# An attention block beside a feed-forward block on one core: truer delays and two new rules in the program that orders the instructions

## The chip, the cores and the metric

The kernel runs on one core of a Trainium2 chip. The metric is device time in microseconds (us). Times are medians of several runs; a run is called fast or slow by its time and by the granted clock of TensorE (the share of its full clock that it was given), which each run records. Ratios are computed as the mean time of one kernel's fast runs over that of the other kernel's fast runs of the same rounds, so they are not quite the ratio of the medians quoted here.

## The reference, cut to what matters

```python
xn = layernorm(x)                              # x: 2048 x 640
q  = xn @ wq   (32 heads of 20)                # one key and one value head for all 32
s  = q k^T * 20**-0.5;  p = softmax(s)         # 32 x 2048 x 2048 scores
A  = (p v) @ wo
B  = relu(xn @ w1 + b1)**2 @ w2 + b2           # F = 1536
out = x + A + B
```

The 134 million exponentials of the softmax are the large item. Most are done by ScalarE; a part is done by VectorE and GpSimd with a bit trick, to relieve ScalarE.

## The kernel before

The order of the instructions is not written by hand. When the kernel is built, a program places every operation on its engine with an assumed duration and assumed delays, always choosing what can start next, and writes the resulting fixed order with semaphores. So wrong figures in this *order model* cannot make a wrong result; they make a poor order. The model is only the ordering program's belief; every time in this text is from the chip.

These terms are used below:

- A **step** is one exponential: ScalarE reads 128x1024 scores from two banks of PSUM, the memory that TensorE writes its products into (`ps` in the trace lines). Its **score pair** (`QK`) is the two TensorE products that filled them. There are two pairs of banks, so pair j must wait until exponential j-2 has been read out, and exponential j must wait for pair j.
- A **set** is a key tile that VectorE handles instead of ScalarE, with 4 score products (`DQK`). Such a product is meant to **ride** directly behind a score pair, because both use a 20-row strip of the array (`20*128` in the trace lines); what changing to other work costs is measured below.
- **Column groups** are all other TensorE work (PV products, which multiply the probabilities by the values; projections; feed-forward): groups of four 32-column products side by side. A **zero-fill** is a group that adds zeros; it is meant to keep the array active (e9 below measures what two such groups were worth at one place).
- A **block** is four heads for 512 queries (32 blocks). Its PV products add up in one bank. When a block ends, this bank is closed until VectorE has transposed it (0.71 us a transpose, from the page).

The parts that the change and the argument touch:

```python
class Op:
    ...
    def ready(self):                          # when the order model believes it can start
        t = 0.0
        for d in self.deps:
            ...
            t = max(t, d.fin + (self.lat1 if self.lat1 is not None and d.eng == "PE" else d.lat))
        return t                              # d.lat: 0.2 from TensorE, 2.2 from a DMA, else 0.06
...
    def make_act(st_):                        # the exponential of a step
        ...
        return Op(f"ACT{st_['j']}", "ACT", 0.064 + 0.4267 * n, [...], deps)
...
    def make_dqk(heads):                      # heads: row groups that the pair just placed occupies
        ...
        h = ([h for h in s["left"] if h not in heads] or s["left"])[0]
        ...
        return Op(f"DQK{d}", "PE", 0.02 if heads else 0.215, [...], ..., mode="R"), s, h, bank
...
    while True:                               # place the next operation
        ...
        for u in active.values():             # "misc units": projections, feed-forward, in chunks
            ...
            consider("PE", 2, o, ("misc", u))
        ...
        if pick[2].eng == "PE":
            ...
            while pick[0] > free["PE"] + 0.1 + (...) and act_ops and pe_use(min(pick[0], free["PE"] + 1.0)) < 1.0:
                ...                           # place a zero-fill, if a bank is open for it
```

Note `0.02 if heads else 0.215`: the model counts a riding product as nearly free, also where `h` is a row group that the pair occupies, that is, where no other head of the set was left. I call that a **colliding rider**. A rider placed after other work, not directly behind its pair, is a **late rider**; the model counts it as nearly free too.

The softmax here doesn't subtract the row's maximum and nothing guards it: scores larger than these inputs give would overflow.

Of the kernel before, what the change touches and what calls it, by code (L numbers as in the profile page):

```python
# [9 lines left out]
AF = mybir.ActivationFunctionType  # L10

S, D, H, DH, F = 2048, 640, 32, 20, 1536
ST, DT, FT, QC, KT = 16, 5, 12, 4, 16
HPG = 4
G = H // HPG
NBLK = QC * G
# [34 lines left out]
QLEAD = 1.98  # L51
RIDE = 0.1
D1LAT = 0.4
ACT_ROWS = (3, 4, 5)
TE_ACT = (0, 1)
TM_POOL = range(NBLK - 1)
# [50 lines left out]
class Op:  # L107
# [23 lines left out]
    def ready(self):  # L131
        t = 0.0
        for d in self.deps:
            if d.fin is None:
                return None
            t = max(t, d.fin + (self.lat1 if self.lat1 is not None and d.eng == "PE" else d.lat))
        return t


def bass_parallel_sum__grouped_kv_mqa__dense_activation_squared_relu__prompt_kernel(nc, A_x, A_wq, A_wk, A_wv, A_wo, B_x, B_w1, B_b1, B_w2, B_b2, out):  # L140
    es = ExitStack()
    with es:
# [504 lines left out]
        def make_act(st_):  # L647
            i0, n = st_["i0"], len(st_["tiles"])
            s0 = i0 % PTR
            deps = [st_["qk"]] + st_["fill"] + [pv_of[act_tiles[i - PTR][:2]] for i in range(i0, i0 + n) if i >= PTR]  # L650
            b0 = st_["banks"][0]
            return Op(f"ACT{st_['j']}", "ACT", 0.064 + 0.4267 * n, [lambda e: e.activation(out=PT[:, s0:s0 + n, :], in_=ps[:, b0:b0 + n, :], func=AF.Exp, bias=-EXP_SHIFT, scale=SCALE)], deps)  # L652

        def after_act(st_):
            for k, t in enumerate(st_["tiles"]):
# [105 lines left out]
        def after_dqk(o, s, h, bank):  # L761
            i = len(s["order"])
            s["left"].remove(h)
            s["order"].append(h)
            n_dqk[0] += 1
            q_users.setdefault(s["b"], []).append(o)
            n = s["n"]
            a = n % NSET
            old = sets[n - NSET] if n >= NSET else None
            olds = sets[n - 2] if n >= 2 else None  # L770
            l = s["d1"][-1] if s["d1"] else None
            if l is not None and l.fin is None and l.banks[-1] + 1 == bank and len(l.banks) < MERGE:
                d1 = l
                d1.banks += (bank,)
                d1.deps.append(o)
                d1.dur = 0.153 + 0.533 * len(d1.banks)
            else:
                d1 = q(Op(f"D1_{n}_{i}", "DVE", 0.686, [], [o] + (old["u"] + old["w"] + old["t"] + old["s"] if old else x_read)), P_D1)
                d1.lat1, d1.banks = D1LAT, (bank,)
                s["d1"].append(d1)  # L780
            bank_last[bank] = d1
            nb, b0 = len(d1.banks), d1.banks[0]
            cs = slice((i + 1 - nb) * 512, (i + 1) * 512)
            d1.parts = [lambda e: e.tensor_scalar(out=lbuf[a][:, cs].bitcast(U16), in0=ps[:, b0:b0 + nb, :].rearrange("p a n -> p (a n)"), scalar1=XA, scalar2=XB, op0=ALU.mult, op1=ALU.add)]  # L784
            if i < HPG - 1:
                return
            X, W, T, M = lbuf[a], wbuf[a], tbuf[a], sbuf[n % 2]
            s["w"] = [dv(f"W{n}", 0.74, lambda e: e.tensor_scalar(out=W.bitcast(U16), in0=X.bitcast(U16), scalar1=0xFF80, scalar2=None, op0=ALU.bitwise_and),  # L788
                         s["d1"] + ([("pv", old, "w")] if old else x_read), P_W, True)]
            s["u"] = [dv(f"U{n}", 0.74, lambda e: e.tensor_scalar(out=T.bitcast(U16), in0=X.bitcast(U16), scalar1=0x7F, scalar2=0x3F80, op0=ALU.bitwise_and, op1=ALU.bitwise_or),  # L790
                         s["d1"] + ([("pv", old, "t")] if old else x_read), P_T, True)]
            s["t"] = [dv(f"T_{n}", 1.235, lambda e: e.tensor_tensor(out=T, in0=X, in1=T, op=ALU.mult), s["u"], P_T)]  # L792
            sdep = s["d1"] + ([("pv", olds, "s")] if olds else x_read)
            if SPOOL[n % len(SPOOL)]:
                for k in range(2):
                    ks = slice(k * 1024, (k + 1) * 1024)
                    s["s"].append(dv(f"S_{n}", 1.06, lambda e, ks=ks: e.tensor_scalar(out=M[:, ks].bitcast(U16), in0=X[:, ks].bitcast(U16), scalar1=float(XS), scalar2=1.0, op0=ALU.add, op1=ALU.mult), list(sdep), 4, True, (), "POOL"))  # L797
            else:
                s["s"].append(dv(f"S_{n}", 0.74, lambda e: e.tensor_scalar(out=M.bitcast(U16), in0=X.bitcast(U16), scalar1=float(XS), scalar2=1.0, op0=ALU.add, op1=ALU.mult), sdep, P_W))
            for term in ("w", "t", "s"):  # L800
                pv_ready[s["b"]].append(("D", (s, term)))
# [5 lines left out]
        def pe_use(t):  # L807

            r = 9.0
            for w, least in UTIL:  # L810
                u = 0.0
                for s_, f_, c_ in reversed(pe_iv):
                    if f_ <= t - w:
                        break
                    u += (min(f_, t) - max(s_, t - w)) * c_ / (f_ - s_)
                r = min(r, u / w / least)
            return r
# [15 lines left out]
        while True:  # L833
            best = {}

            def consider(eng, prio, op, ap):
                if not resolve(op):
                    return
                r = op.ready()
                if r is None:  # L840
                    return
                best.setdefault(eng, []).append((start_of(op, r, False), prio, op, ap))
# [38 lines left out]
            for u in list(misc[:8]):  # L881
# [6 lines left out]
                active[u.bank] = u  # L888
                misc.remove(u)
            for u in active.values():  # L890
                dur, ch = u.chunks[u.k]
                deps, toks = [], []
                if u.k == 0:
                    deps = list(u.deps()) + [bank_last.get(u.bank)]
                    toks = list(u.toks)
                o = Op(f"{u.name}.{u.k}", "PE", dur, ch(u.bank), deps, toks, lat=0.2)
                if u.name == "QT0":
                    o.t0 = 10.0
                consider("PE", 2, o, ("misc", u))
# [5 lines left out]
                consider("POOL", o.prio, o, ("pool",))  # L905
            if sp_q:
                consider("SP", 0, sp_q[0], ("sp",))
            pick = None
            for eng, c in best.items():
                s0 = min(x[0] for x in c)  # L910
# [5 lines left out]
            if pick[2].eng == "PE":  # L916
                if not act_ops and pick[0] > free["PE"] + 0.3:
                    for _ in range(min(6, int((pick[0] - free["PE"]) / 0.22))):
                        commit(Op("warm", "PE", 0.215, [lambda e: e.matmul(ps[:, PVBS[0], :], ones_bf[:, :], hT_tmp[:, 0, :], start=True, stop=True)]))  # L919
                while pick[0] > free["PE"] + 0.1 + (0.2 if pick[2].mode == "R" and pe_mode[0] == "R" else 0.0) and act_ops and pe_use(min(pick[0], free["PE"] + 1.0)) < 1.0:  # L920
                    b_ = pv_blk[0]
                    in_pv = b_ < NBLK and b_ in pv_begun
                    fb = [(x, bank_last[x]) for x in DBANKS if x not in active and bank_last[x].fin is not None and bank_last[x].fin + 0.1 <= free["PE"]]
                    if NPV <= b_ < NBLK and not in_pv and tn_op[b_ - NPV].fin is not None and tn_op[b_ - NPV].fin + 0.1 <= free["PE"]:
                        fb = [(PVBS[b_ % NPV], tn_op[b_ - NPV])]
                    sa = steps[act_next] if act_next < len(steps) and steps[act_next]["qk"].fin is not None else None
                    if not in_pv and not fb and sa is not None and free["PE"] + 0.1 + 0.215 + 0.2 <= free["ACT"]:
                        bk = sa["banks"][len(sa["tiles"]) - 1]
                        f_ = Op("fill", "PE", 0.215, [(lambda e, jj=jj, bk=bk, sa=sa, n=len(sa["fill"]): mm(ps[32 * jj:32 * jj + 32, bk, :], zeros32[:, :], kT[:, 0:512], False, n == len(sa["fill"]) - 1, (0, 32 * jj))(e)) for jj in range(4)],
                                [], [(c_pool, v_zeros)])  # L930
                        commit(f_)
                        sa["fill"].append(f_)
                        if sa["act"] is not None:
                            sa["act"].deps.append(f_)
                        continue
                    if not in_pv and not fb:
                        break
                    bk = PVBS[b_ % NPV] if in_pv else fb[0][0]
                    f_ = Op("fill", "PE", 0.215, [mm(ps[32 * jj:32 * jj + 32, bk, :], zeros32[:, :], kT[:, 0:512], not in_pv, not in_pv, (0, 32 * jj)) for jj in range(4)],
                            [] if in_pv else [fb[0][1]], [(c_pool, v_zeros)])  # L940
                    commit(f_)
# [192 lines left out]
```

## Time and profile before

| what, before | value | read from |
|---|---|---|
| time | 791.91 us, 3 runs (791.35 to 794.25) | runs |
| profiled span | 789.7 us | page |
| exponentials | 810, floor 0.904 us start to start | starts in the trace |
| first exponential starts | 16.15 us | timeline |
| time above the floor, from the 25th on | 24.6 us | starts in the trace |
| from the last exponential's start to the end | 11.7 us | starts in the trace |

"Time above the floor" is the sum, over all exponentials, of the start-to-start time less 0.904 us. I call it *lateness*. It is the part of ScalarE's time that a better order can remove.

From the page of the kernel before: the granted clock in 40 slices, and two of the groups of instructions (line, engine, operation, output and input, count | busy us, mean ns | idle us before, and what ended most of it).

```profile
PEclk9999999999999999999999999999999999999999
...
L652 ACT ACTIVATE PT<-ps 128x1024 bf16<-128x1024 f32 x810 | 752.9, 1051 | 11.1 <-PE ps L308 8.5
...
L308 PEld LDWEIGHTS ps<-qT,kT 20*128 20x128 bf16 x2048 | 80.1, 91 | 297.9 <-ACT PT L652 241.2
```

ScalarE is busy for 96% of the span. Its idle time ended mostly with score products, so the score products came late. The last line seems to say that TensorE has time to spare: its weight loads for the scores waited 241 us for ScalarE. Both are true, at different moments. The timeline of TensorE in the kernel before shows how (start, duration, engine, line, operation, output and inputs, sizes, number of products):

```profile
243.27 0.39 PE L308 MATMUL ps<-qT,kT 20*128 20x512 bf16 x2
243.59 0.40 PE L308 MATMUL ps<-PT,vx 128*32 128x512 bf16 x4
243.82 0.45 PE L308 MATMUL ps<-wo_pad,OTn 128*32 128x320 bf16 x8
244.19 0.39 PE L308 MATMUL ps<-qT,kT 20*128 20x512 bf16 x2
244.51 0.40 PE L308 MATMUL ps<-xnT,wq_sb 128*20 128x512 bf16 x4
244.84 0.38 PE L308 MATMUL ps<-qT,kT 20*128 20x512 bf16 x1
245.15 0.39 PE L308 MATMUL ps<-xnT,wq_sb 128*20 128x512 bf16 x4
245.48 0.60 PE L308 MATMUL ps<-qT,kT 20*128 20x512 bf16 x3
```

Lines with `qT,kT` are score products. The pairs start at 243.27, 244.19 and 245.48 us. Between the last two lie two column groups, as between many pairs, but also a single score product at 244.84. The stretch before it, with three column groups and no rider, takes 0.92 us; this one takes 1.29 us. ScalarE's timeline shows the price:

```profile
242.75 2.90 ACT L652 ACTIVATE PT<-ps 128x1024 bf16<-128x1024 f32 x3
246.12 1.02 ACT L652 ACTIVATE PT<-ps 128x1024 bf16<-128x1024 f32 x1 [0.47 <-PE ps L308]
```

The costs (medians of the trace): pair to first column group 0.32 us; column group to the next 0.23 us for 512 columns and 0.14 us for 320; last group to the next pair 0.32 us (0.24 us at 320 columns). So changing between row strips and column groups costs about 0.10 us each time (0.32 against 0.23 us, 0.24 against 0.14 us). The trace shows this cost, not what makes it. A rider in a row group of its own moves the following group by only 0.003 us (0.321 against 0.318 us). A colliding rider starts 0.23 us after the pair and the next group 0.30 us after it, 0.21 us more in all.

### The profile page before, as it was taken

Reading aid. Unit: us, or ns where it says so; the run is one execution under the profiler, and the core shown is the slowest. Engines: PE = TensorE matmul, PEld = TensorE weight load, DVE = VectorE, ACT = ScalarE, POOL = GpSimd, SP = SyncE. Lnnn points to the kernel's source line nnn. Section 1 sums busy time; section 2 is a strip of 40 time slices with the busy share of each in tenths; the row PEclk is TensorE's granted clock in tenths of the full one; section 3 lists DMA queues with packets and bytes.
Section 4 is the critical chain, followed back from the end, with each engine's and each line's share of the span. In section 5 each row is a group of like instructions: output and inputs, shape, how many; then the busy total and the mean of one; then the engine's idle time right before and its main releaser. Section 6 shows DMA issues by size and latency. Waiting matters only on the chain.

```text
span 789.7 us, 22849 instructions
## 1 busy us (share of the span) xinstructions
PE 776.8 (98%) x10294; PEld 238.3 (30%) x10294; DVE 662.8 (84%) x981; ACT 761.1 (96%) x827; POOL 319.0 (40%) x327
## 2 busy tenths in 40 slices
PE   8999999999999999999999999999999999999997
PEld 3332222222233333322223333322222333332333
DVE  7678989888988888888888888888888888888885
ACT  5899999999999999999999999999999999999994
POOL 5244464453433334335443333335553333333331
PEclk9999999999999999999999999999999999999999
DMA  9500000000000000000000000000000000000001
GB/s 316 137 2 2 1 2 2 2 2 2 1 2 19 10 11 18 2 18 2 2 1 3 18 18 19 2 19 1 2 2 2 19 3 18 19 18 2 3 2 35
DMA packets 11716, 14.95 MB, mean 19 GB/s; under 512 B 2017, under 2 KB 10978, under 8 KB 11618
## 3 DMA queue, kind: packets, MB, share of 16 engines
q1 hardware_dynamic: 10306, 13.44, 5.5%
q8 instruction: 80, 1.31, 0.7%
q10 hardware_dynamic: 1312, 0.05, 0.1%
q14 instruction: 18, 0.15, 0.1%
HBM read 10.87 MB, written 2.62 MB: 17 GB/s over the span
## 4 chain that ended last, share of the span: by engine, by line
PE 72%; ACT 26%; DVE 1%; DMA 1%; issue 0%; SPq 0%; DVEq 0%
PE ps L308 71%; ACT PT L652 25%; DMA x_sb<-in_A_x_dram 1%; DVE Tn L698 0%; DVE out_sb L1009 0%; PE ps L420 0%; ACT PT L344 0%; ACT PT L341 0%; DVE x_sb L784 0%; ACT xnT L393 0%; SPq L226 0%; DVE T L700 0%; ACT qT L448 0%; PE ps L919 0%; DVE w_sb L546 0%
## 5 line engine op out<-in xcount | busy, mean ns | idle before, releaser
L652 ACT ACTIVATE PT<-ps 128x1024 bf16<-128x1024 f32 x810 | 752.9, 1051 | 11.1 <-PE ps L308 8.5
L797 POOL TENSOR_SCALAR dextra<-x_sb 128x1024 uint16<-128x1024 uint16 x214 | 220.7, 1047 | 341.3 <-DVE dextra L790 211.2
L308 PE MATMUL ps<-qT,kT 20*128 20x512 bf16 x2048 | 335.6, 384 | 5.1 <-ACT PT L652 3.9
L784 DVE TENSOR_SCALAR x_sb<-ps 128x512 uint16<-128x512 f32 (+1 forms) x364 | 277.4, 775 | 72.7 <-PE ps L308 71.5
L308 PEld LDWEIGHTS ps<-qT,kT 20*128 20x128 bf16 x2048 | 80.1, 91 | 297.9 <-ACT PT L652 241.2
L308 PE MATMUL ps<-PT,vx 128*32 128x512 bf16 x1620 | 161.7, 389 | 0.3 <-ACT PT L652 0.2
L792 DVE TENSOR_TENSOR dextra<-x_sb,dextra 128x2048 bf16<-128x2048 bf16 x107 | 132.7, 1240 | 0.0
L308 PE MATMUL ps<-w_sb,big 128*32 128x320 bf16 x1536 | 83.6, 301 | 0.0
L308 PE MATMUL ps<-xnT,w_sb 128*32 128x512 bf16 x960 | 79.8, 382 | 0.1
L790 DVE TENSOR_SCALAR dextra<-x_sb 128x2048 uint16<-128x2048 uint16 x107 | 73.2, 685 | 0.0
L308 PEld LDWEIGHTS ps<-PT,vx 128*32 128x32 bf16 x1620 | 41.5, 93 | 96.3 <-issue 94.5
L474 POOL TENSOR_TENSOR big<-hT_tmp 128x512 bf16<-128x512 bf16 x48 | 49.9, 1041 | 44.0 <-DVE dextra L792 19.0
L308 PE MATMUL ps<-kT,zeros 128*32 128x512 bf16 x780 | 67.2, 383 | 0.0
L308 PE MATMUL ps<-wo_pad,OTn 128*32 128x320 bf16 x1024 | 55.1, 301 | 0.6 <-DVE w_sb L546 0.6
L308 PE MATMUL ps<-xnT,wq_sb 128*20 128x512 bf16 x640 | 53.1, 381 | 0.0
L700 POOL TENSOR_TENSOR T<-Tn 128x512 bf16<-128x512 f32 x31 | 34.3, 1107 | 42.2 <-DVE Tn L699 16.1
L788 DVE TENSOR_SCALAR x_sb<-x_sb 128x2048 uint16<-128x2048 uint16 x72 | 50.2, 697 | 0.3
L308 PEld LDWEIGHTS ps<-w_sb,big 128*32 128x32 bf16 x1536 | 35.0, 96 | 30.0 <-issue 18.2
L308 PE MATMUL ps<-dextra,vxt 128*32 128x512 bf16 x428 | 42.0, 383 | 0.0
L308 PE MATMUL ps<-dextra,vxs 128*32 128x512 bf16 x428 | 41.7, 383 | 0.0
L466 DVE TENSOR_SCALAR hT_tmp<-ps,b1col 128x512 bf16<-128x512 f32 x48 | 35.3, 736 | 6.4 <-PE ps L308 6.3
L698 DVE STREAM_TRANSPOSE Tn<-ps 128x512 f32<-128x512 f32 x32 | 22.8, 714 | 12.3 <-PE ps L308 12.2
(69 smaller groups left out, 353.9 us busy)
## 6 DMA issues: line engine op xcount, KB each, us to landing
w_sb<-in_B_w_dram SPq DMA_DIRECT2D x2, 1920.0 KB, 16.3
xr<-in_A_x_dram SPq DMA_DIRECT2D x16, 160.0 KB, 2.4
out_dram<-out_sb SPq DMA_DIRECT2D x16, 160.0 KB, 1.8
x_sb<-in_A_x_dram SPq DMA_DIRECT2D x3, 640.0 KB, 8.8
wq_sb<-in_A_wq_dram SPq DMA_DIRECT2D x1, 800.0 KB, 7.6
wo_pad<-in_A_wo_dram SPq DMA_DIRECT2D x4, 200.0 KB
x_sb<-in_A_x_dram SPq DMA_DIRECT2D x2, 320.0 KB, 3.9
wk_c<-in_A_wk_dram ACTq DMA_DIRECT2D x1, 25.0 KB, 3.7
```

The source lines that it names most:

```text
L308: return lambda e: e.matmul(out_, l, r, start=start, stop=stop, tile_position=tp)
L466: o = q(Op(f"RL{qc}_{f}", "DVE", 0.75, [lambda e: e.tensor_scalar(out=hT_tmp[:, k % 2, :], in0=ps[:, bk, :], scalar1=b1col[:, f:f + 1], sc ...
L474: sq = q(Op(f"SQ{qc}_{f}", "POOL", 1.05, [lambda e: e.tensor_tensor(out=h2T[:, qc % 2, f, :], in0=hT_tmp[:, k % 2, :], in1=hT_tmp[:, k % 2 ...
L652: return Op(f"ACT{st_['j']}", "ACT", 0.064 + 0.4267 * n, [lambda e: e.activation(out=PT[:, s0:s0 + n, :], in_=ps[:, b0:b0 + n, :], func=AF ...
L698: tn = Op(f"TN{b}", "DVE", 0.72, [lambda e: e.transpose(out=Tn[:, a, :], in_=ps[:, PVBS[b % NPV], :])], [lastpv, tm_op.get(b - 2)])
L700: tm = Op(f"TM{b}", *(("POOL", 1.1) if b in TM_POOL else ("DVE", 0.69)), [lambda e: e.tensor_tensor(out=T2[:, a, :].rearrange("p (c d) -> ...
L784: d1.parts = [lambda e: e.tensor_scalar(out=lbuf[a][:, cs].bitcast(U16), in0=ps[:, b0:b0 + nb, :].rearrange("p a n -> p (a n)"), scalar1=X ...
L788: s["w"] = [dv(f"W{n}", 0.74, lambda e: e.tensor_scalar(out=W.bitcast(U16), in0=X.bitcast(U16), scalar1=0xFF80, scalar2=None, op0=ALU.bitw ...
L790: s["u"] = [dv(f"U{n}", 0.74, lambda e: e.tensor_scalar(out=T.bitcast(U16), in0=X.bitcast(U16), scalar1=0x7F, scalar2=0x3F80, op0=ALU.bitw ...
L792: s["t"] = [dv(f"T_{n}", 1.235, lambda e: e.tensor_tensor(out=T, in0=X, in1=T, op=ALU.mult), s["u"], P_T)]
L797: s["s"].append(dv(f"S_{n}", 1.06, lambda e, ks=ks: e.tensor_scalar(out=M[:, ks].bitcast(U16), in0=X[:, ks].bitcast(U16), scalar1=float(XS ...
```

## The change

Its intent: do not start TensorE work that would make the next score pair late for ScalarE; give the order model measured delays, so that it knows when that is; and near the end of a block hold back the rest of a misc unit, so that TensorE has work while the PV bank is closed. The diff, cut to its core:

```diff
+LAT_PE = 0.21
+LAT_ACT = 0.17
+LATE = 0.05
+HOLD = 1
+KEEP = 5
...
-            t = max(t, d.fin + (self.lat1 if self.lat1 is not None and d.eng == "PE" else d.lat))
+            if d.eng == "PE":
+                lat = 0.0 if self.eng == "PE" else (self.lat1 if self.lat1 is not None else LAT_PE)
+            elif d.eng == "SP":
+                lat = d.lat
+            elif self.eng == "PE":
+                lat = LAT_ACT if d.eng == "ACT" else 0.2
+            else:
+                lat = 0.085
+            t = max(t, d.fin + lat)
...                                            # the exponential's assumed time
-  Op(f"ACT{st_['j']}", "ACT", 0.064 + 0.4267 * n, ...)
+  Op(f"ACT{st_['j']}", "ACT", 0.051 + 0.4267 * n, ...)
...
-                d1.lat1, d1.banks = D1LAT, (bank,)
+                d1.lat1, d1.banks = (D1LAT if o.dur < 0.1 else LAT_PE), (bank,)
...                                            # the hold
+                if act_ops and not startup[0] and pv_blk[0] < NBLK - 1 and pv_blk[0] in pv_begun and pv_count[pv_blk[0]] >= KT - HOLD and len(u.chunks) - u.k <= KEEP:
+                    continue
...                                            # the rule
+            limit = 1e9
+            nq = pend[0]["qk"].ready() if ... else None
+            if nq is not None and act_ops:
+                limit = max(nq, free["ACT"] + (...) - LAT_PE - 0.215) + LATE
+                keep = [x for x in best["PE"] if ... or x[0] + x[2].dur + (...) <= limit]
+                best["PE"] = keep
...                                            # and for the zero-fills
-                while pick[0] > free["PE"] + ... < 1.0:
+                while pick[0] > free["PE"] + ... < 1.0 and free["PE"] + 0.215 + SWITCH <= limit:
```

So there are three parts: the **delays**, the **rule** and the **hold**.

More of the change, by code (lines that the diff above doesn't have):

```diff
@@ L651, in make_act @@
             b0 = st_["banks"][0]
-            return Op(f"ACT{st_['j']}", "ACT", 0.064 + 0.4267 * n, [lambda e: e.activation(out=PT[:, s0:s0 + n, :], in_=ps[:, b0:b0 + n, :], func=AF.Exp, bias=-EXP_SHIFT, scale=SCALE)], deps)
+            return Op(f"ACT{st_['j']}", "ACT", 0.051 + 0.4267 * n, [lambda e: e.activation(out=PT[:, s0:s0 + n, :], in_=ps[:, b0:b0 + n, :], func=AF.Exp, bias=-EXP_SHIFT, scale=SCALE)], deps)
         def after_act(st_):
@@ L907, in bass_parallel_sum__grouped_kv_mqa__dense_activation_squared_relu__prompt_kernel @@
                 consider("SP", 0, sp_q[0], ("sp",))
+            limit = 1e9
+            nq = pend[0]["qk"].ready() if pend[0] is not None and any(x[3][0] == "qk" for x in best.get("PE", [])) else None
+            if nq is not None and act_ops:
+                limit = max(nq, free["ACT"] + (0.904 if act_next < pend[0]["j"] else 0.0) - LAT_PE - 0.215) + LATE
+                keep = [x for x in best["PE"] if x[3][0] in ("qk", "dqk") and x[2].dur < 0.1 or x[3][0] == "qk" or x[0] + x[2].dur + (SWITCH if x[2].mode == "C" else 0.0) <= limit]
+                best["PE"] = keep
             pick = None
@@ L919, in bass_parallel_sum__grouped_kv_mqa__dense_activation_squared_relu__prompt_kernel @@
                         commit(Op("warm", "PE", 0.215, [lambda e: e.matmul(ps[:, PVBS[0], :], ones_bf[:, :], hT_tmp[:, 0, :], start=True, stop=True)]))
-                while pick[0] > free["PE"] + 0.1 + (0.2 if pick[2].mode == "R" and pe_mode[0] == "R" else 0.0) and act_ops and pe_use(min(pick[0], free["PE"] + 1.0)) < 1.0:
+                while pick[0] > free["PE"] + 0.1 + (0.2 if pick[2].mode == "R" and pe_mode[0] == "R" else 0.0) and act_ops and pe_use(min(pick[0], free["PE"] + 1.0)) < 1.0 and free["PE"] + 0.215 + SWITCH <= limit:
                     b_ = pv_blk[0]
```

## The prediction

> **What bounds the kernel now.** The groups of instructions show ScalarE doing 810 exponentials of 128x1024. Their start-to-start time has a floor of 0.904 us, so 731 us of the 789.7 us span are ScalarE at its floor. The same starts give 30.6 us above the floor between the first and last exponential: about 6 us of it at start-up (most before the 17th and 25th exponential, waiting for the next key chunks), 24 us after that, about 4 us of which is a second grain of 0.921 us. TensorE reads 98% busy, which says little [...]: in the waits, weight loads wait 242 us for ScalarE.
>
> The timeline shows why the gaps come. The score pair of step j starts at least 1.07 us after exponential j-2 started, and exponential j starts 0.43 us after the pair; 1.50 against 1.81 us for two exponentials leaves 0.30 us of slack. Between two pairs, work costs 0.32 us (into other groups), 0.22 us per 512-column group (0.14 at 320 columns) and 0.32 us back: two groups 0.86, three 1.08. A DVE score product riding on a pair is nearly free unless it uses a row group the pair occupies; then it costs 0.21 us more.
>
> **What the change does.** The order comparison shows 816 exponentials instead of 810, 104 sets on VectorE instead of 107, 416 DVE score products instead of 428, and 196 zero-fill groups against 195. So ScalarE gets six more exponentials: 6 x 0.904 = +5.4 us, all on the critical path.
>
> In return the order should have fewer late pairs. I summed each pair-to-pair stretch with the durations above and ran the lateness against 0.904 us per exponential, an estimate from the trace's durations. For the old order from the 25th exponential on it gives 20.4 us, and with the 4 us of grain this meets the measured 24 us, so TensorE's order alone explains the gaps. For the new order it gives 16.4 us, only 4.0 us less: three-group stretches remain, and colliding riders, whose cost the order model still does not know, rise from 70 to 77. The better wait figures gain little more, since almost no gap comes from other engines.
>
> Tail: 33 instead of 20 projection groups follow the last score pair: about 1.8 us more TensorE, some of it hidden in the 0.6 us wait there; +1.2 us. Start-up: the first exponential comes about 1.4 us later (an extra normalisation and statistics pair precede the key eviction), the gap before the 17th shrinks and that before the 25th grows; together about 0, within 1.5 us.
>
> **Sum.** 791.9 + 5.4 - 4.0 + 1.2 = 794.5; shaded to 793.5 us, since the sum may miss some benefit. Range 788 to 798.5. Faster by over 2%: 0.01; within 2%: 0.975; slower: 0.015.
>
> **What would show it.** Right: 816 exponentials at a 0.904 us floor; time above the floor falling from 30.6 to about 25-28 us; remaining gaps still behind three-group stretches and colliding riders; granted clock still 1.0. Wrong: excess below 20 us (then faster than before), or a clock below 1.0.
>
> **What would make it wrong.** Riders or fills placed with true delays may stop stalling TensorE more than I credit; start-up may shift by more than 1.5 us; the held unit could make TensorE idle and pile work into the tail.

## The result, and the profile after

The changed kernel takes 792.95 us (4 runs, 792.86 to 793.32) against 791.75 us (4 runs). The ratio is 1.0009 with a 95% interval of 0.9989 to 1.003: no difference. All four runs were fast, at a clock of 0.999 or 1.0.

From the page after, the lines that answer to those of before:

```profile
PEclk9999999999999999999999999999999999999999
...
L665 ACT ACTIVATE PT<-ps 128x1024 bf16<-128x1024 f32 x816 | 754.2, 1072 | 8.2 <-PE ps L321 6.9
...
L321 PEld LDWEIGHTS ps<-qT,kT 20*128 20x128 bf16 x2048 | 80.7, 91 | 302.1 <-ACT PT L665 269.6
```

There are six exponentials more, and less idle time before them. Because nothing else sets the length, the span can be cut at the starts of the first, the 25th and the last exponential (us; each number from the trace):

| piece | before | after | difference |
|---|---|---|---|
| start of the span to the first exponential | 16.15 | 18.09 | +1.94 |
| first to 25th | 27.69 | 26.72 | -0.97 |
| 25th to last: exponentials x 0.904 | 709.64 | 715.06 | +5.42 |
| 25th to last: lateness | 24.58 | 17.98 | -6.60 |
| last exponential's start to the end | 11.66 | 13.40 | +1.74 |
| span | 789.72 | 791.26 | +1.54 |

The change did what it was made for: 6.6 us of lateness are gone. Almost all of that is spent on six more exponentials, because fewer sets find their way to VectorE (104 instead of 107), and the rest on the two ends.

The ends can be read from ScalarE's timeline, before and then after (in brackets: the idle time before, and its releaser):

```profile
16.15 7.44 ACT L652 ACTIVATE PT<-ps 128x1024 bf16<-128x1024 f32 x8 [1.13 <-PE ps L308]
24.41 7.44 ACT L652 ACTIVATE PT<-ps 128x1024 bf16<-128x1024 f32 x8 [0.82 <-PE ps L308]
34.66 7.44 ACT L652 ACTIVATE PT<-ps 128x1024 bf16<-128x1024 f32 x8 [2.81 <-PE ps L308]
43.84 1.94 ACT L652 ACTIVATE PT<-ps 128x1024 bf16<-128x1024 f32 x2 [1.74 <-PE ps L308]
```

```profile
18.09 7.44 ACT L665 ACTIVATE PT<-ps 128x1024 bf16<-128x1024 f32 x8 [1.59 <-PE ps L321]
25.81 7.44 ACT L665 ACTIVATE PT<-ps 128x1024 bf16<-128x1024 f32 x8 [0.28 <-PE ps L321]
34.34 7.44 ACT L665 ACTIVATE PT<-ps 128x1024 bf16<-128x1024 f32 x8 [1.09 <-PE ps L321]
44.81 1.02 ACT L665 ACTIVATE PT<-ps 128x1024 bf16<-128x1024 f32 x1 [3.04 <-PE ps L321]
```

Each group of 8 exponentials waits for the next keys. In TensorE's and VectorE's timelines before, for instance, the products of the key projection start at 40.86 us, `kT` is written from 42.17 us, the score products start at 43.41 and the exponential at 43.84 us. The later first start is made good by the third group; then a longer wait before the 25th makes the start 0.97 us slower after all.

Which stretches hold the lateness? With the order of the products taken from the ordering program, I put each start-to-start time over 0.93 us down to the TensorE work between its score pair and the one before (from the 25th exponential on, the last ten left out; us, and number of gaps):

| the stretch holds | before | after |
|---|---|---|
| a colliding rider | 9.4 (52) | 6.6 (46) |
| a late rider | 2.8 (12) | 3.2 (14) |
| three or more 512-column groups, no such rider | 5.4 (57) | 3.9 (48) |
| something else | 2.7 (32) | 1.6 (18) |

This puts a name to each gap; whether the named thing is the cause is for the experiments.

### The profile page after: what moved, and what is told of

Read it like the earlier page. It is cut to its first block, busy times and chain, and to the rows that moved or that the text cites. A ratio compares the mean times of both kernels' runs of the same rounds, so it can differ in the third digit from the quotient of the medians.

```text
span 791.3 us, 22788 instructions
## 1 busy us (share of the span) xinstructions
PE 779.6 (99%) x10277; PEld 237.4 (30%) x10279; DVE 653.4 (83%) x953; ACT 762.4 (96%) x833; POOL 311.9 (39%) x321
## 4 chain that ended last, share of the span: by engine, by line
PE 56%; ACT 43%; DVE 0%; issue 0%; POOL 0%; DVEq 0%; POOLq 0%
PE ps L321 54%; ACT PT L665 43%; PE ps L279 1%; PE ps L941 0%; PE ps L400 0%; DVE out_sb L1031 0%; PE ps L433 0%; ACT qT L461 0%; DVE w_sb L559 0%; POOL hT_tmp L247 0%; DVEq L155 0%; POOL ones_bf L245 0%; POOL scr L249 0%; POOLq L1141 0%
## 5 line engine op out<-in xcount | busy, mean ns | idle before, releaser
L810 POOL TENSOR_SCALAR dextra<-x_sb 128x1024 uint16<-128x1024 uint16 x208 | 213.8, 1043 | 341.4 <-DVE dextra L803 236.9
L797 DVE TENSOR_SCALAR x_sb<-ps 128x512 uint16<-128x512 f32 (+1 forms) x345 | 268.9, 792 | 81.6 <-PE ps L321 79.7
L805 DVE TENSOR_TENSOR dextra<-x_sb,dextra 128x2048 bf16<-128x2048 bf16 x104 | 130.3, 1253 | 0.0
L321 PE MATMUL ps<-wo_pad,OTn 128*32 128x320 bf16 x1024 | 57.6, 301 | 0.6 <-DVE w_sb L559 0.6
```

Source lines behind the costliest of these rows:

```text
L321: return lambda e: e.matmul(out_, l, r, start=start, stop=stop, tile_position=tp)
L797: d1.parts = [lambda e: e.tensor_scalar(out=lbuf[a][:, cs].bitcast(U16), in0=ps[:, b0:b0 + nb, :].rearrange("p a n -> p (a n)"), scalar1=X ...
L805: s["t"] = [dv(f"T_{n}", 1.235, lambda e: e.tensor_tensor(out=T, in0=X, in1=T, op=ALU.mult), s["u"], P_T)]
L810: s["s"].append(dv(f"S_{n}", 1.06, lambda e, ks=ks: e.tensor_scalar(out=M[:, ks].bitcast(U16), in0=X[:, ks].bitcast(U16), scalar1=float(XS ...
```

## The experiments

**Theory 1.** TensorE's order makes the lateness. The delays made it better, and also took the three sets from VectorE; the rule and the hold did little. What is left comes above all from riders that the model counts as free. **Rival to theory 1:** the rule is what helped, or the lateness is waiting for other engines. All runs gave correct results; "full clock" means a granted clock of 0.998 or more. The runs were made on four chips (e1 to e4 on chip 3, e5 to e8 on chip 5, e9 to e11 on chip 12, e12 on chip 2), each with the kernel before in the same rounds.

### The three parts apart: e1, e2, e3, e10

e1 keeps only the delays, e2 only the rule, e3 delays and rule, e10 delays and hold. The switches:

```diff
 # no rule
-                limit = max(...) + LATE
+                limit = max(...) + 1e6
 # no hold
-KEEP = 5
+KEEP = -1
 # no delays: the lines of ready(), make_act and d1.lat1 as before the change
```

> The changed kernel with the order rule and the hold switched off; only the measured delays stay. Order: 816 exponentials, 104 VectorE sets, 38 projection groups after the last score pair (changed kernel: 33). Theory 1 (the delays make both the six extra exponentials and most of the lower lateness; the rule adds little): 816 exponentials, time above 0.904 us from the 25th exponential on 18 to 21 us, total 793 to 797 us. Rival (the rule that leaves TensorE free is what lowered the lateness): lateness stays at 23 to 26 us, total 798 to 801 us.

> The changed kernel with the old delays and without the hold; only the rule that leaves TensorE free stays. Order: 810 exponentials, 107 VectorE sets, 93 colliding riders (before 70), 40 projection groups at the end. Theory 1: with wrong delays the rule aims at the wrong moment and the lateness does not fall: 24 to 29 us from the 25th exponential on, total 795 to 801 us. Rival (the rule is what lowers the lateness): lateness 18 us at 810 exponentials, total 785 to 789 us.

> The changed kernel without the held misc unit. Order: 816 exponentials, 104 sets, 67 colliding riders (with the hold 77), 13 projection groups after the last score pair instead of 33. Theory 1 (the hold only shifts work): lateness 17 to 19 us, tail shorter by 1.5 to 3 us, total 789 to 792 us. Rival (the hold frees the PV bank at each block's end and so saves lateness): lateness 20 us or more and total 793 us or more.

> The changed kernel without the rule that leaves TensorE free: measured delays and hold. Order: 816 exponentials, 73 colliding riders, 24 projection groups at the end, 3 score pairs with no work behind them (15 in e1, which is the same kernel without the hold). Theory 2 (the hold keeps work for the time in which the PV bank is closed, and so keeps the clock): clock 1.0 in all runs, unlike e1; lateness 16 to 19 us; total 790.5 to 793.5 us. Rival (it is the rule that keeps the clock): clock under 0.98 in some runs and a median over 800 us.

In e1 the clock fell late in the profiled run, so all are compared over the 25th to the 761st exponential, which lie before that fall. "Bare pairs" are score pairs from the 25th on that have no column group behind them in the order; they matter further down.

| kernel | delays | rule | hold | exponentials | lateness, 25th to 761st | bare pairs | time, median | granted clock of the runs |
|---|---|---|---|---|---|---|---|---|
| before | | | | 810 | 23.0 | 6 | 791.5 to 791.9 | mostly 0.999 to 1.0, a few 0.986 to 0.997 |
| e2 | | x | | 810 | 22.7 | 10 | 798.02 | 0.997, 0.980, 0.999, 0.987 |
| e1 | x | | | 816 | 16.9 | 15 | 820.3 | 0.951, 0.969, 0.999, 0.883 |
| e3 | x | x | | 816 | 16.7 | 7 | 790.54 | 0.999 to 1.0 |
| e10 | x | | x | 816 | 17.0 | 3 | 791.38 | 0.999 |
| after | x | x | x | 816 | 16.9 | 2 | 792.95 | 0.999 to 1.0 |

The delays alone bring both the six exponentials and the whole fall in lateness, from 23.0 to 16.9 us. The rule alone changes it by 0.3 us, and on top of the delays by 0.2 us. In this column the hold does nothing either. In e3, without the hold, the end of the kernel is 2.7 us shorter (10.7 instead of 13.4 us), since 13 instead of 33 groups are left over after the last pair.

What nobody expected stands in the last column. e1 at full clock took 793.72 us, within its expectation, but three of its four runs lost the clock and took up to 880.66 us. e2 took 793.6 us in its one full-clock run; I had expected 795 to 801. Its profiled run had a fall of 3.4 us at 21.3 us, in the start-up. So an order that is as good by lateness can be far slower, and the rule and the hold may be worth something after all. This is taken up below.

### Riders that are not free: e4, e5, e6

e4 is the changed kernel, but lets a product ride only in a row group of its own:

```diff
+            if heads and all(h in heads for h in s["left"]):
+                return None
             h = ([h for h in s["left"] if h not in heads] or s["left"])[0]
```

> The changed kernel, but a VectorE score product rides on a pair only where it has a row group of its own; otherwise it waits for the next pair. Order: no colliding riders (77 in the changed kernel), 818 exponentials, 103 sets, 15 projection groups at the end. Theory 1 (the lateness that is left comes from TensorE's own order, above all from collisions the order model counts as free): lateness from the 25th exponential on falls from 18 to 4 to 8 us, total 780 to 786 us. Rival (what is left is waiting for other engines, or for the exponential's own release): lateness stays 16 to 19 us, and with two more exponentials the total is 792 to 796 us.

e5 also forbids late riders:

```diff
+            if o.eng == "PE" and o.mode == "C":
+                heads[0] = []
             if kind == "act":
```

> As e4, and a VectorE score product may ride only directly behind a score pair, not after other TensorE work. Order: 818 exponentials, no colliding and no late riders, 22 projection groups at the end. Theory 1 (TensorE's order makes the lateness; the trace of e4 puts 3.4 us of its 11.8 us on stretches with a late rider): lateness from the 25th exponential on 5 to 9.5 us, total 780 to 785 us. Rival (late riders only fill time that was free): lateness 11 to 13 us, total 786 to 788 us.

e6 puts both edits into the kernel *before*, with nothing of the change.

> The kernel before, with none of the change, and with the two rider rules of e5. Order: 816 exponentials, 105 sets or fewer, no colliding and no late riders, 5 projection groups at the end. Theory 1 (before's lateness was 9.4 us behind colliding and 2.8 us behind late riders): lateness falls from 24.6 to 10 to 14 us although no delay is measured, start as before, total 780 to 785 us. Rival (without true delays the order puts something else late): lateness over 18 us, total 788 us or more.

| kernel | exponentials | lateness from the 25th on | time, median | ratio to before |
|---|---|---|---|---|
| after | 816 | 18.0 | 792.95 | 1.0009 |
| e4 | 818 | 11.8 | 786.28 (4 runs, 786.21 to 786.32) | 0.9917 (0.9894 to 0.994) |
| e5 | 818 | 9.9 | 785.87 (4 runs, 785.68 to 786.14) | 0.9919 (0.9903 to 0.9935) |
| e6 | 816 | 11.6 | 783.13 and 785.88 at clocks of 1.0 and 0.994; 840.45 and 840.58 at 0.916 | fast runs: 0.9901 |

e4 removes 6.2 us of lateness, and the colliding riders had been put down for 6.6 us. So there the named thing was the cause. The rival expected 16 to 19 us and falls. Taking away the late riders as well brings only 1.9 us more, where I had put 3.4 us down to them. e6 shows the same without any measured delay: 24.6 becomes 11.6 us, a larger step than the change itself made.

My figures for e4 (4 to 8 us, up to 786 us) and e5 (5 to 9.5 us, up to 785 us) were missed on the high side. The sum that I had used for them counts a stretch of three 512-column groups as harmless when the one before leaves room. In e5's trace 67 stretches with three or more 512-column groups are still late, by some 0.08 us each and 5.3 us in all, and the sum had called most of these free. No run here tells why.

### The clock: e7, e8, e9

e7 is the changed kernel with the late-rider edit alone; e8 is e5 without the hold and with `LATE = 0.0`.

> The changed kernel with the late-rider rule alone; collisions stay (78). Order: 816 exponentials, 34 projection groups at the end. Theory 1 (late riders cost 3.2 us in the changed kernel's trace): lateness from the 25th exponential on 13 to 16 us (changed kernel 18.0), total 788.5 to 791.5 us. Rival: lateness 17 us or more, total 792 us or more.

> As e5, without the held unit and with the allowed lateness of the rule cut from 0.05 to 0. Order: 818 exponentials, 14 projection groups at the end. Theory 1: lateness 5 to 9 us, tail near 10.8 us, total 779 to 783.5 us, the fastest so far. Rival (a TensorE left free more often loses its clock, as in e1): mean granted clock under 0.99 in some runs and times spread by over 5 us.

Both came out far slower: e7 takes 833.01 us (829.52 to 836.74; clock 0.933 to 0.941 in all four runs), e8 810.12 us (798.7 to 860.28; clock 0.892 to 0.978). For e8 that is what the rival said; for e7 neither had it. e7's runs agree with each other, but at a low clock; they must not be compared with full-clock runs as if only the order differed. The granted clock of e7 and e8, from their pages:

```profile
PEclk9999999999999999999999999999755555999999
```

```profile
PEclk9999557999999999999999999999969999999999
```

The clock records in these traces are either 1.0 or 0.5. In e7 it is 0.5 from 593.4 us for 112.6 us, in e1 from 734.5 us for 78.5 us, in e8 from 80.5 us for 51.2 us and from 589.1 us for 13.7 us; the fall in e2's start-up lasted 3.4 us. What ended these stretches, the runs do not show: TensorE counts as 100% busy in them where I asked (e7 from 600 to 700 us, e1 from 740 to 800 us). TensorE's timeline in e7 just before its fall:

```profile
590.20 0.39 PE L321 MATMUL ps<-qT,kT 20*128 20x512 bf16 x2
590.52 0.40 PE L321 MATMUL ps<-PT,vx 128*32 128x512 bf16 x4
591.12 0.39 PE L321 MATMUL ps<-qT,kT 20*128 20x512 bf16 x3 [0.20 <-ACT PT L665]
592.03 0.39 PE L321 MATMUL ps<-qT,kT 20*128 20x512 bf16 x2 [0.53 <-ACT PT L665]
592.95 0.39 PE L321 MATMUL ps<-qT,kT 20*128 20x512 bf16 x2 [0.53 <-ACT PT L665]
593.27 0.54 PE L321 MATMUL ps<-PT,vx 128*32 128x512 bf16 x4
593.58 0.65 PE L321 MATMUL ps<-x_sb,vx 128*32 128x512 bf16 x4
594.00 0.65 PE L321 MATMUL ps<-dextra,vxt 128*32 128x512 bf16 x4
```

A block has just ended at 590.52. Its PV bank is closed, no other bank is open for a zero-fill, and no misc unit can start (the one at hand waits for a bank). Pairs 618 and 619 (591.12 and 592.03) stand alone: no column group runs from 590.92 to 593.27 us, while a score pair is issued every 0.91 us or so. Then products of 512 columns take 0.65 instead of 0.39 us. Counting each product's rows, columns and length against full 128x128 products at 0.216 us per 512 columns (the spacing of such products in the warm-up at the start of the trace before, once it had fallen from 0.427 us, 4.2 us after the first of them), and each product whole at its start, I estimate that in the 1.7 us (a window of my choice) up to 592.9 us the array did 4% of what it could; e8's falls at 80.5 and 589.1 us follow such windows of 4% and 8%. The mean over either run is about 54% and 55%, an estimate from the 447 us of full products that the same count gives for the traces before and after, over spans of 835.0 and 809.7 us. All these places are ends of blocks. e1's fall at 734.5 us also follows two thin pairs at the end of a block, but with 20% in the window; and the same trace has windows of 8% at 150 and 382 us and of 10% at 711 us, after which the clock stayed at 1.0.

**Theory 2.** The clock is lost where a few neighbouring pairs stand alone. **Rival:** it is the average load of the order, or the chip. e9 adds to e7 one zero-fill group of four small products behind each of the two lone pairs, into the pair's own bank, and leaves the rest of the order untouched (a comparison of the orders shows exactly those 8 products more):

```diff
+PAD = (618, 619)
...                                            # the last product of the pair no longer closes its group
+            if j in PAD:
+                parts += [mm(ps[32 * jj:32 * jj + 32, banks[len(tl) - 1], :], zeros32[:, :], kT[:, 0:512], False, True, (0, 32 * jj)) for jj in range(4)]
```

> e7 with nothing changed in its order but two zero-fill groups (4 small matmuls each) added right behind the two neighbouring score pairs 618 and 619, which had no other TensorE work behind them. In e7's trace the clock fell to a half at 593.4 us, just after these two. Theory 2 (the clock falls because these two stretches leave the array almost without work): the clock stays at 1.0, lateness from the 25th exponential on 13 to 16 us, total 788.5 to 792 us instead of 833. Rival (the clock falls from the average load of the order, or from the chip): falls again, total over 810 us.

e9 takes 788.72 us (788.62 to 788.96), the clock is 1.0 in all four runs, and the ratio to before is 0.9945 (0.9902 to 0.9989). The same place in e9:

```profile
590.12 0.39 PE L322 MATMUL ps<-qT,kT 20*128 20x512 bf16 x2
590.44 0.40 PE L322 MATMUL ps<-PT,vx 128*32 128x512 bf16 x4
591.04 0.39 PE L322 MATMUL ps<-qT,kT 20*128 20x512 bf16 x2 [0.20 <-ACT PT L669]
591.36 0.40 PE L322 MATMUL ps<-kT,zeros 128*32 128x512 bf16 x4
591.69 0.65 PE L322 MATMUL ps<-qT,kT 20*128 20x512 bf16 x3
592.28 0.40 PE L322 MATMUL ps<-kT,zeros 128*32 128x512 bf16 x4
592.89 0.39 PE L322 MATMUL ps<-qT,kT 20*128 20x512 bf16 x2 [0.22 <-ACT PT L669]
593.21 0.40 PE L322 MATMUL ps<-PT,vx 128*32 128x512 bf16 x4
```

And the windows view of both, e7 first (stretch and its length; busy us and number of instructions of PE, PEld, DVE, ACT and POOL; granted clock; DMA share, GB/s):

```profile
590.00:600.00 10.00, 8.74 (x70) 1.68 (x63) 8.51 (x13) 7.66 (x9) 3.09 (x3) 0.67 0.01 2
600.00:700.00 100.00, 100.00 (x813) 21.59 (x809) 47.95 (x69) 63.63 (x63) 20.69 (x20) 0.50 0.03 8
```

```profile
590.00:600.00 10.00, 9.58 (x110) 2.57 (x110) 10.00 (x16) 9.93 (x12) 4.46 (x5) 1.00 0.01 2
600.00:700.00 100.00, 99.61 (x1429) 31.54 (x1433) 84.10 (x120) 99.89 (x110) 35.78 (x35) 1.00 0.04 12
```

Eight small products that compute nothing are worth 44 us. In the slow hundred microseconds TensorE counts as 100% busy while it does 813 products instead of 1429, and ScalarE gets through 63 exponentials instead of 110. By the count used above, an estimate, the array did 33% of what it could while e7's clock was down, against 57% at the same place in e9. So the average load of the order is out for e7: eight products do not change it. A difference between chips is not quite out, since e7 ran on chip 5 and e9 on chip 12. But the kernel before and e5 kept the clock at 0.995 or more on chip 5 in the same rounds, and chip 12 is not immune: there the kernel before fell to 0.987 in one run, and e11 (below) lost the clock too. With the fall gone, e7's own question has an answer too: without late riders the lateness is 13.6 us instead of 18.0, inside the 13 to 16 us expected.

This suggests what the hold is worth. The kernels e1 and e10 differ in the hold alone: 15 bare pairs and falling clocks in three of four runs without it, 3 bare pairs and 0.999 in every run with it, though on another chip. The rule without the hold was enough as well (e3: 7 bare pairs, full clock, on e1's chip and in its rounds). So with the delays either of the two went with a kept clock, in four runs each; that they kept it by having fewer bare pairs is not shown, since e1's only recorded fall came at 20%. At full clock the hold gains no time; in the changed kernel it costs 2.7 us of tail (e3).

Bare pairs do not tell everything. e3 has a window of 8% in its trace (126.3 us) and still kept the clock in all four runs; e8 lost it at 8%, e1 at 20%, and e6, with 12 single bare pairs, in two of four runs. So theory 2 is shown for the one place in e7. That a lone pair makes a fall likelier elsewhere is plausible and not shown, and a fall also depends on something that differs between runs of one kernel (e6's four have clocks of 1.0, 0.994, 0.916 and 0.916). What, these runs do not show.

### A faster version: e11 and e12

e11 is e5 with a higher priority for the score evictions among VectorE's operations (which brings two sets back: 105 instead of 103) and with padding behind its 7 bare pairs.

```diff
-P_D1 = 2
+P_D1 = 0
+PAD = (24, 312, 313, 464, 465, 514, 515)
```

> e5 with the score evictions of VectorE put first among its operations, and a zero-fill group behind each of the 7 score pairs that have no other work behind them. Order: 814 exponentials (e5: 818), 105 sets, no colliding and no late riders, 19 projection groups at the end. Theories 1 and 2 together: clock 1.0, lateness 9 to 12 us, four exponentials fewer than e5 (-3.6 us), total 779.5 to 783.5 us, the fastest that is steady. Rival (fewer exponentials only move the wait to VectorE's sets): lateness 13 us or more, total 785 us or more.

e12 pads 13 more pairs (its expectation says 12; the list in the kernel has 20 in all): the neighbours, and places where two neighbouring stretches hold one group each.

> e11 with zero-fill groups behind 19 score pairs instead of 7: the 12 added ones are their neighbours and other places where two neighbouring stretches hold one work group each. The rest of the order is e11's. Theory 2 (e11's two slower runs, at clocks of 0.986 and 0.981, lost the clock in such thin stretches): clock 0.995 or more in all runs, total 781.5 to 783.5 us. Rival (they lost it elsewhere, for example at start-up[...]): some runs again at 0.98 to 0.99 and 786 us or more.

e11 took 782.02 and 782.04 us at full clock, but 788.91 and 794.6 us at clocks of 0.986 and 0.981. At full clock it has four exponentials fewer than e5 and the same lateness (10.0 us), as theory 1 has it. e12 is steady, 785.5 to 786.22 us in six runs at 0.998 to 1.0 (ratio 0.9917, interval 0.9888 to 0.9945), but missed its expected time: its lateness is 13.8 us. All the new pads stand in front of a group that was there already, where the pair's completion then comes later: 13 exponentials each wait 0.16 to 0.44 us longer than in e11. In these runs padding was free only behind a pair with nothing behind it (e11: 10.0 us of lateness against e5's 9.9). That e11 lost its clock in the places that e12 pads is possible, with six full-clock runs against two of four. But the two ran on different chips, no profile fell into a slow run of e11, and its full-clock trace has no 1.7 us window under 20% after the start-up, so it is not shown.

The fastest steady versions are e5 and e12 at 785.9 and 785.7 us, 0.8% under the kernel before; e4 (786.3 us) and e9 (788.7 us) are steady too. e11 is 1.2% under the kernel before (782.0 against 791.7 us) while the clock holds.

## Why the prediction was right, point by point

- **Time.** Predicted 793.5 us, range 788 to 798.5; measured 792.95.
- **The bound.** Right. ScalarE's floor of 0.904 us and TensorE's order make up the span; e4 and e6 moved the time by editing only where TensorE's riders may stand.
- **Six exponentials, +5.4 us.** Right: 816, and 5.42 us. The cause was left open; e1 shows that the delays alone bring them.
- **Lateness, -4.0 us.** The sign was right, the size was not: -6.6 us. Of the difference, 1.5 us is the small grain (start-to-start times near 0.921 instead of 0.904 us), which I took as fixed at 4 us and which fell from 4.2 to 2.7 us; the rest is 5.1 instead of 4.0 us in the larger gaps. So "time above the floor falling from 30.6 to about 25-28 us" was also wrong: it fell to 23.0 us.
- **Riders.** Right that colliding riders are the largest part of what remains (e4). Wrong in suggesting that their rise from 70 to 77 costs more: the gaps behind them fell from 9.4 to 6.6 us, as more of them stand where there is room.
- **Tail, +1.2 us.** Measured +1.74 us. The step that failed is "some of it hidden in the 0.6 us wait there": that wait is still there (0.61 before, 0.60 us after).
- **Start-up, 0 within 1.5 us.** Measured +0.97 us. The three shifts named (first later, gap before the 17th smaller, before the 25th larger) all happened; the first was 1.9 instead of 1.4 us.
- **The sum came out well because misses cancelled:** 2.6 us too little gain against 1.5 us too little cost at the ends. The net of 1.1 us is about what the shading from 794.5 to 793.5 us had allowed for, without naming a source. That the result lies so near is luck in this part.
- **What the prediction took for granted:** the clock. It expected 1.0, rightly, but not that the rule and the hold might matter for it. It said that the hold could make TensorE idle. e1 against e10 points the other way: with the hold, fewer pairs stand alone (3 instead of 15). In the result itself nothing of this shows, because the changed kernel has all three parts and keeps its clock.

## What to carry to other kernels

When an order is made by a model, look first for costs that the model counts as zero: here two rider edits of two lines each took 8 us off the lateness, more than exact delays and a look-ahead rule together. Cutting a wait pays only after counting what the new order puts on the bottleneck engine: six more exponentials ate nearly all of the gain. And where runs show TensorE's clock falling, as e7's did (0.933 to 0.941), look at the thinnest two microseconds of the order too, and not only at the average: eight empty products in one such place were worth 44 us. Not every thin place loses the clock (e1, e3), and not every loss here was traced to one (e6, e11).
